# Quarters of turned operands change places in one round of transfers, and the first two groups are loaded once

## The chip, the core and the metric

The kernel runs on one core of a Trainium2 chip. Time is device time of one execution, in microseconds (us), lower is better. Five engines run their own instruction streams in order: TensorE (PE, matmuls), VectorE (DVE), ScalarE (ACT), GpSimd (POOL) and SyncE (SP, which here only issues transfers). Sixteen DMA engines carry the transfers of all queues.

## The reference

Sigmoid attention and two gated MLPs, in float32 (some weights come as float64):

```
scores = q @ k.T / sqrt(64) - log(448)          # q, k, v: 4 batches, 12 heads, 448 x 64
x  = sigmoid(scores) @ v                        # heads side by side: 4 x 448 x 768
h  = relu(x @ w_in);  u, v = halves of h        # 768 -> 2 x 512
x  = (u * (w_spatial @ layernorm(v) + b)) @ w_out
h  = gelu(x @ w_in2); u, v = halves of h
out = x + (u * (w_sg @ (layernorm(v) * g) + b2)) @ w_out2
```

## The kernel before, in words

The work runs in two parts. The first is attention; both MLPs follow, and their matmuls leave PE no gap. The change touches attention alone (the function `attention`).

Attention takes the 48 heads in 12 groups of four. A group has 7 units, one for each 64 keys, so there are 84 units. `scores(n, c)` issues four matmuls for unit c of group n, one for each head, each on a quarter of PE's array (64 rows by 64 columns), and then the sigmoid on ACT. `values(n, c)` issues four more, which add the unit's part to the group's output. In the loop, step s issues the scores of unit s and the values of unit s - LAG, with LAG = 4. In the trace each matmul has two records, so one such set of four is eight records. I call it a **set**. ACT (`gather`) copies a finished group out.

The operands of `scores` need the 64 elements of a head's rows on 64 partitions. `load(n)` brings q and k of a group as 128 rows (4 heads x 32), and `transpose` turns 32x32 blocks on DVE, which puts only 32 elements of each head on 32 partitions of a tile. So `turn(n)` makes two tiles, `even` (elements 0 to 31) and `odd` (32 to 63), and then exchanges quarters: `even[32:64]` (head 1) and `odd[0:32]` (head 0) change places, and so do the quarters 64 partitions on. It copies `even` into a spare tile (L415), sends two transfers from `odd` to `even` (L417), and, because the second pair overwrites what the first reads, sends two more from the spare to `odd` once the first have landed (L419). POOL issues these four transfers. There is one buffer for the spare (`bufs=1`), so the copy of the next group waits until the last pair has landed. There are three buffers for each operand tile and four for what is loaded.

The first two groups go another way: `load_twice` loads each head's rows twice, the second time shifted by 32 elements, so that the transposes (`turn_twice`) put both halves where they belong and nothing is exchanged. SP and ACT issue these loads.

The order of the work is written out: `turn(n + 2)` stands at unit 5 of group n, `load(n + 3)` at unit 3, and `load_v(n + 1)` at unit 0. SP issues q, k and v and the weights of the first MLP in that order, each behind the buffer it fills. On DVE the same program order mixes `turn` with the belt (`convert_early`, L168 to L199): jobs that load a piece of float64 weights and convert it with five to seven DVE instructions; `rate` says when a job starts.

Of the kernel before, what the change touches and what calls it, by code (L numbers as in the profile page):

```python
# [9 lines left out]
F32 = mybir.dt.float32  # L10
# [16 lines left out]
def tile_sigmoid_attention_two_gated_mlps(  # L27
# [32 lines left out]
    nc = tc.nc  # L60
    B, H, S, D = q.shape
    DM = out.shape[2]
    FF = g_ln2.shape[0]
    P = 128
# [3 lines left out]
    TC = S // 32  # L68
# [19 lines left out]
    def chunk_of(b, c):  # L88
        t, c = (xs, c) if c < KF else (xe, c - KF)
        return t[b // 2][:, c * ROW:(c + 1) * ROW + PAD]  # L90
# [253 lines left out]
    for c in range(soon):  # L344
        rows = slice(c * P, (c + 1) * P)
# [7 lines left out]
    def attention(apool, epool, ps_att, ps_last, done):  # L353
        G = H // 4
        NG = B * G

        def place(n):
            b, i = divmod(n, G)
            return b ^ 1, i

        KC = S // 64
        ring, open_sums = [0, 1, 2, 3], {}

        def banks_of(k, name):
            pool = ps_att if k < 3 else ps_last
            return pool.tile([P, 2, 512], F32, tag=f"s{k}", name=name, bufs=1)
        ins, ops, vs, att = {}, {}, {}, {}

        def heads(t, n):
            b, i = place(n)  # L370
            return t[b, 4 * i:4 * i + 4]

        def load_twice(n):


            for w in range(2):
                ins[n, w] = t = apool.tile([P, 2, TC * D], F32, tag="in", name="in", bufs=4)
                src = heads((q, k)[w], n).rearrange("(o x) (t c) d -> o t x (c d)", o=2, c=TC)
                for j in range(2):
                    for o in range(2):  # L380
                        at = 64 * o + 32 * j
                        (nc.sync, nc.scalar)[o].dma_start(
                            out=t[at:at + 32, :, :TC * D - 32 * j], in_=src[o, :, :, 32 * j:]
                        )

        def load(n):
            ins[n] = apool.tile([P, 2, TC * D], F32, tag="in", name="in", bufs=4)
            for w in range(2):
                src = heads((q, k)[w], n).rearrange("h (t c) d -> (h t) (c d)", c=TC)
                nc.sync.dma_start(out=ins[n][:, w], in_=src)  # L390

        def operand(n, x):
            if (n, x) not in ops:
                ops[n, x] = apool.tile([P, 2, S], F32, tag=f"op{x}", name=f"op{x}", bufs=3)
            return ops[n, x]

        def transpose(t, w, src, j=0, chunks=slice(0, None)):
            src = src.rearrange("p (c j d) -> p j c d", c=TC, j=2)[:, j]
            dst = t[:, w]
            if w:  # L400
                src = src.rearrange("p (e c) d -> p c e d", c=KC)[:, chunks]
                dst = dst.rearrange("p (c t e) -> p c e t", c=KC, e=2)[:, chunks]
            else:
                dst = dst.rearrange("p (c t) -> p c t", c=TC)
            nc.vector.transpose(out=dst, in_=src)  # L405

        def turn(n):


            even, odd = [operand(n, x) for x in range(2)]  # L410
            for j, t in enumerate((even, odd)):
                for w in range(2):
                    transpose(t, w, ins[n][:, w], j)
            spare = apool.tile([P, 2, S], F32, tag="ops", name="ops", bufs=1)
            nc.vector.tensor_copy(out=spare, in_=even)  # L415
            for at in (0, 64):
                nc.gpsimd.dma_start(out=even[at + 32:at + 64], in_=odd[at:at + 32])  # L417
            for at in (0, 64):
                nc.gpsimd.dma_start(out=odd[at:at + 32], in_=spare[at + 32:at + 64])  # L419

        def load_v(n):
            vs[n] = vt = epool.tile([P, 2, KC * D], F32, tag="v", name="vt", bufs=3)
            src = heads(v, n)
            row, head = KC * D, S * D
            both = bass.AP(src.tensor, src.offset, [[row, P], [2 * head, 2], [1, row]])
            nc.sync.dma_start(out=vt, in_=both)

        def scores(n, c):


            k = ring.pop(0)
            ring.append(k)
            sc = banks_of(k, "sc")
            for x in range(2):
                for o in range(2):
                    ps, op = slice(64 * o, 64 * o + 64), ops[n, x]
                    nc.tensor.matmul(  # L437
                        sc[64 * x:64 * x + 64, o, :S], op[ps, 1, 64 * c:64 * c + 64], op[ps, 0],
                        start=True, stop=True, tile_position=(64 * o, 64 * x),
                    )  # L440
            att[n, c] = a = epool.tile([P, 2, S], F32, tag="a", name="a", bufs=6)
            nc.scalar.activation(a, sc[..., :S], AF.Sigmoid, bias=bias_s, scale=scale)  # L442

        def values(n, c):


            if n not in open_sums:
                k = ring.pop(0)
                open_sums[n] = k, banks_of(k, "av")
            k, av = open_sums[n]  # L450
            for x in range(2):
                for o in range(2):
                    ps = slice(64 * x, 64 * x + 64)
                    nc.tensor.matmul(  # L454
                        av[o * D:(o + 1) * D, x, :S], vs[n][ps, o, D * c:D * (c + 1)],
                        att[n, c][ps, o], start=(c == 0), stop=(c == KC - 1),
                        tile_position=(64 * x, 64 * o),
                    )
            if c == KC - 1:
                for x in range(2):  # L460
                    gather(n, x, av[:, x])
                ring.append(k)

        def gather(n, x, av):

            b, i = place(n)
            y = chunk_of(b, 2 * i + x)
            o = av[:, :S].rearrange("p (c t) -> p t c", c=TC)

            def back(at, t0, t1):  # L470
                dst = y[:, at:at + (t1 - t0) * TC]
                nc.scalar.copy(out=dst.rearrange("p (t c) -> p t c", c=TC), in_=o[:, t0:t1])

            if b % 2 == 0:
                back(0, 0, 32)
            else:
                t = 3 * P // TC
                back(SPAN, 0, t + 1)
                back(S - 3 * P % TC, t, 32)

        belt.waiting = [convert_early(apool, *x) for x in first]

        units = [(n, c) for n in range(NG) for c in range(KC)]
        U, LAG = len(units), 4

        def rate(p, step):
            if p == 0:
                return int(step in (2, 5))
            return int(step in ((0, 2, 5) if p < NG // 2 - 1 else range(4)))

        load_twice(0)
        load_v(0)
        load_twice(1)
        load(2)
        load_v(1)
        warm = banks_of(ring[-1], "av")[:, 0]
        for _ in range(9):
            nc.tensor.matmul(warm[:, :P], ident, ident, start=True, stop=True)

        def turn_twice(n, w, *chunks):  # L500
            for x in range(2):
                transpose(operand(n, x), w, ins[n, w][:, x], 0, *chunks)

        turn_twice(0, 0)
        for chunks in (slice(0, 1), slice(1, None)):
            turn_twice(0, 1, chunks)
        for s in range(U + LAG):
            n, c = divmod(s, KC)
            if s < U:
                scores(n, c)  # L510
            elif s == U:
                done()
            if s >= LAG:
                values(*units[s - LAG])
            if s in (0, 1):
                turn_twice(1, s)
            if c == 5 and n + 2 < NG:
                turn(n + 2)
            if c == 3 and n + 3 < NG:
                load(n + 3)  # L520
            if c == 0 and 0 < n < NG - 1:
                load_v(n + 1)
            if s % 2 == 0:
                belt.tick(rate(s // 14, s % 14 // 2))
            if s == U:
                load_vecs(l1)
            if s >= U and (s - U) % 2 == 0:
                spatial.tick(1)

        assert open_sums[NG - 1][0] == 3  # L530


    class Mlp:
# [175 lines left out]
        ends = slice(0, 512), slice(512, DM)  # L709
# [103 lines left out]
    with tc.manual_schedule():  # L813
# [4 lines left out]
        apool = tc.tile_pool(name="apool", bufs=1)  # L818
# [13 lines left out]
        with tc.tile_pool(name="epool", bufs=1, side="right") as epool:  # L832
            attention(apool.__enter__(), epool, ps_att.__enter__(), ps_last.__enter__(), operands_made)
# [199 lines left out]
```

## Time and profile before

| | |
|---|---|
| time, median of 3 runs | 579.65 us (577.44 to 581.04) |
| the profiled execution | 580.25 us, span 578.5 us |
| PE busy | 555.5 us, 96% of the span |
| DVE, ACT, POOL busy | 333.5, 219.3, 53.0 us |
| DMA | 62.78 MB, 4.59 MB of them on the queue that POOL issues |
| chain of waits | PE 81%, DMA 13%, other issue 3% |

PE is busy nearly all the time, but this share is a mean over two parts. Where PE has gaps, it is in the first 163 us.

### The profile page before, as it was taken

To read this page: it belongs to the slowest core of one execution; us is meant where nothing else is said; L and a number is where in the kernel's file an instruction comes from. 1 tells how busy PE (TensorE), PEld (TensorE's weight loads), DVE (VectorE), ACT (ScalarE), POOL (GpSimd) and SP (SyncE) were. 2 spreads that over 40 slices of the span, in tenths; PEclk is the share of its full clock that TensorE was granted. 3 is DMA by queue.
4 is the path that set the end of the run, shared out by engine and by line. 5 is a ranking of instruction groups with operands and counts; after the bars stand their busy time and mean duration, and the time that the engine had idled before them with its cause. 6 is when DMAs were issued, how large, how long until landed. Compare 5 with 4: busy or idle time off the path is not lost.

```text
span 578.5 us, 8922 instructions
## 1 busy us (share of the span) xinstructions
PE 555.5 (96%) x3382; PEld 435.9 (75%) x3382; DVE 333.5 (58%) x710; ACT 219.3 (38%) x369; POOL 53.0 (9%) x102
## 2 busy tenths in 40 slices
PE   5959899799999999999999999999999999999997
PEld 4525343233468989889898888999899989999886
DVE  1356675667347969999966597781533065314311
ACT  1726577477744325245253225430321042103101
POOL 0011121212002010020100003000200030001000
PEclk9979899899999999999999999999999999999999
DMA  9996759586233216545345543500230024004103
GB/s 232 316 255 180 199 158 234 134 243 170 76 67 90 91 59 167 121 126 150 95 124 148 130 134 90 153 12 2 37 59 0 1 33 64 1 0 66 17 1 109
DMA packets 90106, 62.78 MB, mean 109 GB/s; under 512 B 63952, under 2 KB 77136, under 8 KB 90064
## 3 DMA queue, kind: packets, MB, share of 16 engines
q1 hardware_dynamic: 88000, 55.56, 37.2%
q0 software_dynamic: 1280, 4.59, 3.2%
q10 hardware_dynamic: 784, 2.06, 1.4%
q8 instruction: 26, 0.43, 0.3%
q14 instruction: 16, 0.13, 0.1%
HBM read 46.60 MB, written 11.01 MB: 100 GB/s over the span
## 4 chain that ended last, share of the span: by engine, by line
PE 81%; DMA 13%; issue 3%; DVE 1%; POOL 0%; SPq 0%; DVEq 0%; POOLq 0%
PE t L562 17%; PE t L608 17%; PE sc L694 10%; PE t L628 6%; DMA op<-ops 6%; PE av L454 5%; PE sc L437 5%; PE av L694 5%; DMA op<-op 4%; PE av L628 3%; PE sc L628 3%; PE sc L704 3%; PE t L790 3%; PE av L790 3%; DMA in<-in_q_dram 2%
## 5 line engine op out<-in xcount | busy, mean ns | idle before, releaser
L437 PE MATMUL sc<-op 64*64 64x448 f32 x672 | 130.5, 573 | 18.2 <-DMA op<-ops 12.9
L454 PE MATMUL av<-a,vt 64*64 64x448 f32 x672 | 124.0, 555 | 0.0
L442 ACT ACTIVATE a<-sc,small 128x896 f32<-128x896 f32 x84 | 84.8, 1013 | 64.7 <-PE sc L437 64.3
L437 PEld LDWEIGHTS sc<-op 64*64 64x64 f32 x672 | 48.9, 142 | 60.5 <-issue 42.7
L454 PEld LDWEIGHTS av<-a,vt 64*64 64x64 f32 x672 | 46.8, 138 | 35.2 <-issue 33.3
L571 DVE BATCH_NORM_STATS2 st<-vr 128x6 f32<-128x512 f32 x28 | 19.4, 694 | 66.8 <-ACT vr L568 66.8
L568 ACT ACTIVATE vr<-t 128x512 f32<-128x512 f32 x28 | 16.7, 597 | 93.9 <-PE t L562 93.9
L573 POOL TENSOR_SCALAR st<-st 128x1 f32<-128x1 f32 x28 | 10.8, 385 | 347.5 <-DVE st L572 347.5
L562 PE MATMUL t<-vh,xh 128*128 128x512 f32 x112 | 41.7, 392 | 0.0
L562 PE MATMUL t<-vh,xl 128*128 128x512 f32 x98 | 38.2, 390 | 0.0
L638 DVE SCALAR_TENSOR_TENSOR gt<-t,bb 128x448 f32<-128x448 f32 x16 | 10.9, 682 | 45.5 <-PE t L628 45.5
L646 ACT CAST gh<-u 128x448 fp32r<-128x448 f32 (+1 forms) x16 | 8.6, 540 | 71.5 <-DVE u L642 71.5
L405 DVE STREAM_TRANSPOSE op<-in 128x448 f32<-128x448 f32 (+2 forms) x50 | 27.2, 599 | 14.7 <-DMA in<-in_q_dram 9.8
L608 PE MATMUL t<-xh,uh 128*128 128x448 f32 x96 | 34.9, 364 | 0.0
L608 PE MATMUL t<-xh,ul 128*128 128x448 f32 x96 | 34.8, 363 | 0.0
L608 PE MATMUL t<-xl,uh 128*128 128x448 f32 x96 | 34.6, 361 | 0.0
L628 PE MATMUL t<-sh,v 128*128 128x448 f32 x112 | 32.8, 363 | 0.0
L562 PE MATMUL t<-vl,xh 128*128 128x512 f32 x84 | 32.7, 390 | 0.0
L550 DVE TENSOR_TENSOR xl<-x,xh 128x512 fp32r<-128x512 f32 (+1 forms) x32 | 20.0, 654 | 20.1 <-ACT xh L549 20.1
L608 PE MATMUL t<-xh,vl 128*128 128x448 f32 x96 | 29.6, 363 | 0.0
L613 ACT ACTIVATE u<-t 128x448 f32<-128x448 f32 x32 | 17.4, 543 | 25.1 <-PE t L608 25.0
L590 ACT CAST v<-vr 128x512 fp32r<-128x512 f32 x24 | 14.9, 622 | 30.5 <-DVE vr L582 30.5
(192 smaller groups left out, 1221.9 us busy)
## 6 DMA issues: line engine op xcount, KB each, us to landing
w<-in_moe_w_in_dram SPq DMA_DIRECT2D x24, 256.0 KB, 2.9
vt<-in_v_dram SPq DMA_DIRECT2D x12, 448.0 KB, 4.6
w<-in_moe_w_out_dram SPq DMA_DIRECT2D x18, 256.0 KB, 3.2
in<-in_q_dram SPq DMA_DIRECT2D x10, 448.0 KB, 6.7
in<-in_k_dram SPq DMA_DIRECT2D x10, 448.0 KB, 8.0
we<-in_moe_w_in_dram SPq DMA_DIRECT2D x12, 256.0 KB, 10.7
we<-in_moe_w_in_dram SPq DMA_DIRECT2D x16, 192.0 KB, 7.3
out_dram<-y SPq DMA_DIRECT2D x48, 56.0 KB, 1.9
```

Of the source, the lines that this page charges most:

```text
L405: nc.vector.transpose(out=dst, in_=src)
L437: nc.tensor.matmul(sc[64 * x:64 * x + 64, o, :S], op[ps, 1, 64 * c:64 * c + 64], op[ps, 0], start=True, stop=True, tile_position=(64 * o, ...
L442: nc.scalar.activation(a, sc[..., :S], AF.Sigmoid, bias=bias_s, scale=scale)
L454: nc.tensor.matmul(av[o * D:(o + 1) * D, x, :S], vs[n][ps, o, D * c:D * (c + 1)], att[n, c][ps, o], start=(c == 0), stop=(c == KC - 1), ti ...
L550: nc.vector.tensor_tensor(out=pair[1][:, :n], in0=src, in1=raw(pair[0][:, :n]), op=ALU.subtract)
L562: nc.tensor.matmul(ps[:, :FF], a, w, start=(c == 0 and n == 0), stop=(c == self.kc - 1 and n == 2),)
L571: nc.vector.bn_stats(out=st, in_=vr)
L608: nc.tensor.matmul(ps[:, :S], w, a, start=(c == 0 and n == 0), stop=(c == self.kc - 1 and n == 2),)
L613: nc.scalar.activation(u, ps[:, :S], AF.Relu if L.n == 1 else AF.Gelu_apprx_tanh)
L628: nc.tensor.matmul(ps[:, :S], a, w, start=(n == 0), stop=(n == len(todo) - 1))
L694: nc.tensor.matmul(self.o[m][:, :n_cols], w, a, start=(not second and i == 0 and n == 0), stop=(second and i == KF - 1 and n == 2),)
L790: nc.tensor.matmul(ps[:, :FF], x, w[:, c], start=(c == 0 and n == 0), stop=(c == KD - 1 and n == 2),)
```

## The change

There are three edits. First, `turn` makes two copies, one of each operand tile (`spares`, tags `t0` and `t1`, one buffer each), and sends all four transfers from the copies, so that none waits for another. Second, groups 0 and 1 are loaded once like the others, by SP alone. Group 1 exchanges its quarters by four copies on DVE. Group 0 is turned by `turn_first`: its transposes write the spare tiles; the first two units (`EARLY`) take their operands from there, in parts of 32 rows that are added up, so that each of these units has eight score matmuls instead of four; meanwhile DVE, ACT and POOL put the exchanged operands together for the units after. Third, `turn(n + 2)` moves from unit 5 to unit 2, and LAG becomes 3, with a table (`sums`) for the first steps.

```diff
--- before.py
+++ after.py
@@ -364,35 +364,28 @@
         def banks_of(k, name):
             pool = ps_att if k < 3 else ps_last
             return pool.tile([P, 2, 512], F32, tag=f"s{k}", name=name, bufs=1)
-        ins, ops, vs, att = {}, {}, {}, {}
+        ins, ops, vs, att, early, EARLY = {}, {}, {}, {}, [], 2
 
         def heads(t, n):
             b, i = place(n)
             return t[b, 4 * i:4 * i + 4]
-
-        def load_twice(n):
-
-
-            for w in range(2):
-                ins[n, w] = t = apool.tile([P, 2, TC * D], F32, tag="in", name="in", bufs=4)
-                src = heads((q, k)[w], n).rearrange("(o x) (t c) d -> o t x (c d)", o=2, c=TC)
-                for j in range(2):
-                    for o in range(2):
-                        at = 64 * o + 32 * j
-                        (nc.sync, nc.scalar)[o].dma_start(
-                            out=t[at:at + 32, :, :TC * D - 32 * j], in_=src[o, :, :, 32 * j:]
-                        )
 
         def load(n):
             ins[n] = apool.tile([P, 2, TC * D], F32, tag="in", name="in", bufs=4)
             for w in range(2):
                 src = heads((q, k)[w], n).rearrange("h (t c) d -> (h t) (c d)", c=TC)
-                nc.sync.dma_start(out=ins[n][:, w], in_=src)
-
-        def operand(n, x):
-            if (n, x) not in ops:
-                ops[n, x] = apool.tile([P, 2, S], F32, tag=f"op{x}", name=f"op{x}", bufs=3)
-            return ops[n, x]
+                ends = (0, 9 * D, TC * D) if (n, w) == (0, 1) else (0, TC * D)
+                for cols in map(slice, ends, ends[1:]):
+                    nc.sync.dma_start(out=ins[n][:, w, cols], in_=src[:, cols])
+
+        def operands(n):
+            ops[n] = [
+                apool.tile([P, 2, S], F32, tag=f"op{x}", name=f"op{x}", bufs=3) for x in range(2)
+            ]
+            return ops[n]
+
+        def spares():
+            return [apool.tile([P, 2, S], F32, tag=f"t{x}", name=f"t{x}", bufs=1) for x in range(2)]
 
         def transpose(t, w, src, j=0, chunks=slice(0, None)):
             src = src.rearrange("p (c j d) -> p j c d", c=TC, j=2)[:, j]
@@ -404,19 +397,48 @@
                 dst = dst.rearrange("p (c t) -> p c t", c=TC)
             nc.vector.transpose(out=dst, in_=src)
 
+        def swaps(ts, us):
+
+
+            for at in (0, 64):
+                yield ts[0][at + 32:at + 64], us[1][at:at + 32]
+                yield ts[1][at:at + 32], us[0][at + 32:at + 64]
+
         def turn(n):
 
 
-            even, odd = [operand(n, x) for x in range(2)]
-            for j, t in enumerate((even, odd)):
+            ts = operands(n)
+            for j, t in enumerate(ts):
                 for w in range(2):
                     transpose(t, w, ins[n][:, w], j)
-            spare = apool.tile([P, 2, S], F32, tag="ops", name="ops", bufs=1)
-            nc.vector.tensor_copy(out=spare, in_=even)
-            for at in (0, 64):
-                nc.gpsimd.dma_start(out=even[at + 32:at + 64], in_=odd[at:at + 32])
-            for at in (0, 64):
-                nc.gpsimd.dma_start(out=odd[at:at + 32], in_=spare[at + 32:at + 64])
+            us = spares()
+            for t, u in zip(ts, us):
+                nc.vector.tensor_copy(out=u, in_=t)
+            for dst, src in swaps(ts, us):
+                if n == 1:
+                    nc.vector.tensor_copy(out=dst, in_=src)
+                else:
+                    nc.gpsimd.dma_start(out=dst, in_=src)
+
+        def turn_first():
+
+
+            ts, us = operands(0), spares()
+            early[:] = us
+            at = ins[0]
+            for j in range(2):
+                transpose(us[j], 0, at[:, 0], j)
+            for j in range(2):
+                transpose(us[j], 1, at[:, 1], j, slice(0, EARLY))
+            for t, u in zip(ts, us):
+                nc.vector.tensor_copy(out=t[:, 0], in_=u[:, 0])
+            for j in range(2):
+                transpose(us[j], 1, at[:, 1], j, slice(EARLY, None))
+            for t, u in zip(ts, us):
+                nc.vector.tensor_copy(out=t[:, 1, 64 * EARLY:], in_=u[:, 1, 64 * EARLY:])
+            for i, (dst, src) in enumerate(swaps(ts, us)):
+                nc.vector.tensor_copy(out=dst[:, 1, 64 * EARLY:], in_=src[:, 1, 64 * EARLY:])
+                (nc.scalar.copy, nc.gpsimd.tensor_copy)[i % 2](out=dst[:, 0], in_=src[:, 0])
 
         def load_v(n):
             vs[n] = vt = epool.tile([P, 2, KC * D], F32, tag="v", name="vt", bufs=3)
@@ -431,13 +453,19 @@
             k = ring.pop(0)
             ring.append(k)
             sc = banks_of(k, "sc")
-            for x in range(2):
-                for o in range(2):
-                    ps, op = slice(64 * o, 64 * o + 64), ops[n, x]
-                    nc.tensor.matmul(
-                        sc[64 * x:64 * x + 64, o, :S], op[ps, 1, 64 * c:64 * c + 64], op[ps, 0],
-                        start=True, stop=True, tile_position=(64 * o, 64 * x),
-                    )
+            parts = [(64, ops[n], 0, 1)]
+            if n == 0 and c < EARLY:
+                parts = [(32, early[j:j + 1] * 2, j, 2) for j in range(2)]
+            for rows, op, j, js in parts:
+                for x in range(2):
+                    for o in range(2):
+                        at = 64 * o if rows == 64 else 64 * o + 32 * x
+                        ps = slice(at, at + rows)
+                        nc.tensor.matmul(
+                            sc[64 * x:64 * x + 64, o, :S], op[x][ps, 1, 64 * c:64 * c + 64],
+                            op[x][ps, 0], start=(j == 0), stop=(j == js - 1),
+                            tile_position=(at, 64 * x),
+                        )
             att[n, c] = a = epool.tile([P, 2, S], F32, tag="a", name="a", bufs=6)
             nc.scalar.activation(a, sc[..., :S], AF.Sigmoid, bias=bias_s, scale=scale)
 
@@ -481,40 +509,35 @@
         belt.waiting = [convert_early(apool, *x) for x in first]
 
         units = [(n, c) for n in range(NG) for c in range(KC)]
-        U, LAG = len(units), 4
+        U, LAG = len(units), 3
+        sums = dict(zip((1, 3, 4), units))
+        sums.update(zip(range(6, U + LAG), units[3:]))
 
         def rate(p, step):
             if p == 0:
                 return int(step in (2, 5))
             return int(step in ((0, 2, 5) if p < NG // 2 - 1 else range(4)))
 
-        load_twice(0)
+        load(0)
         load_v(0)
-        load_twice(1)
+        load(1)
         load(2)
         load_v(1)
         warm = banks_of(ring[-1], "av")[:, 0]
         for _ in range(9):
             nc.tensor.matmul(warm[:, :P], ident, ident, start=True, stop=True)
-
-        def turn_twice(n, w, *chunks):
-            for x in range(2):
-                transpose(operand(n, x), w, ins[n, w][:, x], 0, *chunks)
-
-        turn_twice(0, 0)
-        for chunks in (slice(0, 1), slice(1, None)):
-            turn_twice(0, 1, chunks)
+        turn_first()
         for s in range(U + LAG):
             n, c = divmod(s, KC)
             if s < U:
                 scores(n, c)
             elif s == U:
                 done()
-            if s >= LAG:
-                values(*units[s - LAG])
-            if s in (0, 1):
-                turn_twice(1, s)
-            if c == 5 and n + 2 < NG:
+            if s in sums:
+                values(*sums[s])
+            if s == 0:
+                turn(1)
+            if c == 2 and n + 2 < NG:
                 turn(n + 2)
             if c == 3 and n + 3 < NG:
                 load(n + 3)
```

How the instructions now stand, at three places. Names with a number are buffers: `op0_192` and `op1_193` are the two operand tiles of group 2, `t0_198` and `t1_199` its copies.

POOL, the exchanges of groups 2 and 3 and the first half of the next, before:

```order
L417 DMA op0_206<-op1_207 32x896 x2
L419 DMA op1_207<-ops_212 32x896 x2
L417 DMA op0_316<-op1_317 32x896 x2
L419 DMA op1_317<-ops_322 32x896 x2
L417 DMA op0_434<-op1_435 32x896 x2
```

and now, behind the two copies of group 0:

```order
L441 COPY op1_123<-t0_124 32x448 x2
L421 DMA op0_192<-t1_199 32x896
L421 DMA op1_193<-t0_198 32x896
L421 DMA op0_192<-t1_199 32x896
L421 DMA op1_193<-t0_198 32x896
```

All four read copies, so the third no longer reads or writes what the first two do.

DVE around the exchange of groups 2 and 3, before:

```order
L405 STREAM_TRANSPOSE op1_207<-in_120 128x7x2x32
L415 COPY ops_212<-op0_206 128x896
L175 TENSOR_SCALAR fe_253<-we_192 128x512
L178 TENSOR_SCALAR fe_253<-fe_253 128x512
L181 TENSOR_SCALAR fe_253<-fe_253 128x512
L185 SCALAR_TENSOR_TENSOR fe_253<-we_192,fe_253 128x512
L190 SCALAR_TENSOR_TENSOR fe_253<-we_192,fe_253 128x512
L198 CAST vh1_73<-fe_253 128x512
L199 TENSOR_TENSOR vl1_74<-fe_253,vh1_73 128x512
L405 STREAM_TRANSPOSE op0_316<-in_177 128x448
```

and now (`in_217` is the load of group 3, `we_231` the first piece of weights):

```order
L398 STREAM_TRANSPOSE op1_193<-in_107 128x7x2x32
L416 COPY t0_198<-op0_192 128x896
L416 COPY t1_199<-op1_193 128x896
L175 TENSOR_SCALAR fe_276<-we_231 128x512
L178 TENSOR_SCALAR fe_276<-fe_276 128x512
L181 TENSOR_SCALAR fe_276<-fe_276 128x512
L185 SCALAR_TENSOR_TENSOR fe_276<-we_231,fe_276 128x512
L398 STREAM_TRANSPOSE op0_296<-in_217 128x448
L398 STREAM_TRANSPOSE op0_296<-in_217 128x7x2x32
L398 STREAM_TRANSPOSE op1_297<-in_217 128x448
L398 STREAM_TRANSPOSE op1_297<-in_217 128x7x2x32
L416 COPY t0_302<-op0_296 128x896
```

Two copies stand where one was, and the turn of group 3 comes in the middle of the first weight job instead of behind it.

PE at the start, before:

```order
L498 MATMUL av_125<-ident_63 128x128 x9
L437 MATMUL sc_143<-op0_135 64x448 x2
L437 MATMUL sc_143<-op1_137 64x448 x2
L437 MATMUL sc_154<-op0_135 64x448 x2
L437 MATMUL sc_154<-op1_137 64x448 x2
```

and now:

```order
L528 MATMUL av_112<-ident_63 128x128 x9
L464 MATMUL sc_144<-t0_124 64x448 x4
L464 MATMUL sc_144<-t1_125 64x448 x4
L464 MATMUL sc_169<-t0_124 64x448 x4
L464 MATMUL sc_169<-t1_125 64x448 x4
L482 MATMUL av_180<-a_153,vt_102 64x448 x4
L464 MATMUL sc_185<-op0_122 64x448 x2
```

Units 0 and 1 read the spare tiles with eight matmuls each; the exchanged operands (`op0_122`) are first read by unit 2, behind the values of unit 0.

## Rows read from the trace of the kernel before

**Rows 1.** Busy time by stretches: start:end, length, engines, granted clock, DMA share, GB/s.

```profile
10.79:39.06 28.27, 21.91 (x196) 11.09 (x197) 12.03 (x23) 14.89 (x18) 2.23 (x4) 0.97 1.04 284
39.06:163.23 124.17, 117.61 (x1149) 50.47 (x1149) 75.95 (x156) 81.37 (x106) 18.24 (x36) 0.95 0.65 174
163.23:578.50 415.27, 411.74 (x2021) 370.40 (x2020) 243.93 (x527) 121.56 (x244) 31.80 (x56) 1.00 0.30 74
```

**Rows 2.** Chain of waits, 23 to 54 us: start, length, what.

```profile
23.47 7.07 DMA op<-op
...
31.40 8.60 DMA op<-ops
...
41.32 6.17 DMA op<-op
...
48.55 5.23 DMA op<-ops
```

**Rows 3.** Timeline of PE, where it waited: start, length, instruction, [idle before, releaser].

```profile
39.06 1.99 PE L437 MATMUL sc<-op 64*64 64x448 f32 x3 [6.36 <-DMA op<-ops]
53.82 0.59 PE L437 MATMUL sc<-op 64*64 64x448 f32 x1 [0.86 <-DMA op<-ops]
...
67.33 0.59 PE L437 MATMUL sc<-op 64*64 64x448 f32 x1 [0.99 <-DMA op<-ops]
...
106.02 1.00 PE L437 MATMUL sc<-op 64*64 64x448 f32 x1 [3.13 <-DMA op<-ops]
```

**Rows 4.** Busy time in two stretches of 1 us, columns as in rows 1.

```profile
39.00:40.00 1.00, 0.94 (x2) 0.28 (x2) 0.00 (x0) 0.00 (x0) 0.00 (x0) 0.50 1.03 257
...
107.00:108.00 1.00, 1.00 (x12) 0.32 (x8) 0.93 (x3) 0.13 (x1) 0.70 (x2) 0.50 0.00 0
```

**Rows 5.** Timeline of the start, columns as in rows 3.

```profile
1.35 4.21 PE L498 MATMUL av<-ident 128*128 128x128 f32 x18 [1.35 <-POOL ident masks.py:199]
...
7.11 1.17 DVE L405 STREAM_TRANSPOSE op<-in 128x448 f32<-128x448 f32 x2 [6.22 <-DMA in<-in_q_dram]
...
10.79 6.94 PE L437 MATMUL sc<-op 64*64 64x448 f32 x40 [5.24 <-DVE op L405]
...
12.73 1.01 ACT L442 ACTIVATE a<-sc,small 128x896 f32<-128x896 f32 x1 [10.51 <-PE sc L437]
...
14.22 1.01 ACT L442 ACTIVATE a<-sc,small 128x896 f32<-128x896 f32 x1 [0.49 <-PE sc L437]
...
18.26 0.98 PE L437 MATMUL sc<-op 64*64 64x448 f32 x8
...
30.28 0.98 PE L437 MATMUL sc<-op 64*64 64x448 f32 x8
```

**Rows 6.** Busy time in the first 20 us, columns as in rows 1.

```profile
0.00:4.00 4.00, 2.65 (x12) 2.65 (x13) 0.09 (x2) 1.49 (x2) 0.69 (x6) 1.00 0.55 133
4.00:10.00 6.00, 1.56 (x8) 1.26 (x6) 1.17 (x2) 0.00 (x0) 0.00 (x0) 1.00 1.03 253
10.00:20.00 10.00, 9.21 (x68) 4.79 (x72) 3.74 (x9) 5.64 (x6) 0.00 (x0) 1.00 1.04 290
```

**Rows 7.** Instructions by shape, 0 to 165 us: count, busy us, mean ns, idle before.

```profile
L405 DVE STREAM_TRANSPOSE op<-in 128x448 f32<-128x448 f32 x46 | 25.9, 618 | 12.5 <-DMA in<-in_q_dram 9.8 <-DMA in<-in_k_dram 2.7
...
L415 DVE COPY ops<-op 128x896 f32<-128x896 f32 x10 | 6.2, 619 | 31.9 <-DMA op<-ops 31.9
...
L472 ACT COPY x<-av 128x392 f32<-128x392 f32 x8 | 3.9, 493 | 0.0
...
masks.py:199 POOL TENSOR_SCALAR_AFFINE_SELECT ident<-ident 128x128 f32<-128x128 f32 x1 | 0.3, 292 | 0.1
```

**Rows 8.** Timeline of DVE and POOL, 106 to 110 us, columns as in rows 3.

```profile
106.10 0.63 DVE L415 COPY ops<-op 128x896 f32<-128x896 f32 x1 [7.59 <-DMA op<-ops]
...
107.30 0.98 POOL L417 DMA_DIRECT2D op<-op  x2 [7.63 <-DVE fe L190]
109.89 1.05 POOL L419 DMA_DIRECT2D op<-ops  x2 [1.60 <-PE sc L437]
```

## The prediction

> **What bounds the kernel now.** I read the stages first, then the chain of waits, then what PE waited for, then the prices. From 163.23 us on PE is busy 411.74 of 415.27 us [rows 1]: the MLPs are bound by PE, the change leaves them alone, so whatever the end of attention gains or loses moves the end of the run one for one. In attention the reader is to see two things. The first scores start at 10.79 us, after PE sat idle 5.24 us behind the turned k of group 0 [rows 5]. And the waits of PE are released by the exchange: 6.36 us idle before 39.06, which is unit 14, the first of group 2, and shorter ones before units 21, 28 and 49 at 53.82, 67.33 and 106.02 [rows 3]. In the chain of waits each exchange stands as two rounds, one behind the other: 7.07 and 8.60 us for group 2, 6.17 and 5.23 us for group 3 [rows 2]. The copy into the spare, which must wait until the round before has landed, adds up to 31.9 us of idle DVE [rows 7].
>
> At full pace a unit costs 1.5025 us: the sets of scores at 18.26 and 30.28 us are eight units apart [rows 5]. A unit is two sets, so a set is 0.751 us. At 39.06 the scores of units 14 to 83 (70 sets) and the values of units 10 to 83 (74) are left: 144 x 0.751 = 108.2 us. They took 124.17 us [rows 1]. So 16.0 us are lost behind unit 14, in waits and in the clock after them: the granted clock is 0.50 (1.2 GHz) at 39 us, after 6.36 us idle, and 0.50 at 107 us, after 3.13 us idle [rows 3, 4].
>
> **The change, part by part.** The sum stands on two questions: when unit 14 starts now, and whether anything stops PE behind it.
>
> *Start.* A load of q or k is 448 KB, 0.459 MB. The DMA engines moved 133 GB/s up to 4 us, 253 up to 10 us and 290 up to 20 us at a share of 1.03 to 1.04 [rows 6]: they are full, and the bytes set the times. Of group 0, q was moved twice, 0.90 MB. At these rates that is moved at 5.5 us; the transposes started at 7.11 us [rows 5], so 1.6 us lie between moved and usable. Now q is moved by 3.7 us (the early rate is the least known) and usable at 5.3, the first 9/14 of k at 6.5. The four transposes that unit 0 needs cost 2 x 0.59 for q (1.17 for two [rows 5]) and about 2 x 0.26 for 128 columns of k, by the columns from 0.618 for 448 [rows 7]: first scores near 7.1 us, 3.7 earlier than before.
>
> *Unit 7.* Units 0 and 1 have eight score matmuls each, two sets more. At the start the sigmoids of scores alone stand 1.49 us apart [rows 5], so a set took twice 0.751: PE ran at half pace for about 5.7 us. If it does so again, 3.8 sets are done by 12.8 us. Unit 7 needs 9 sets of scores and 4 of values in front of it, so 9.2 more: 19.7 us. Its operands: DVE does the rest of group 0 (two copies of 448 columns, two transposes and two copies of 320, four copies of 320 columns) at 0.619 for 896 columns and 0.618 for a transpose of 448: 0.66 + 0.94 + 0.5 + 1.0, done at 10.2 us. Group 1 has landed when 2.29 MB are moved, 10.8 + 1.6 = 12.4 us; behind it three transposes, two copies and four copies of 896 columns are 1.85 + 1.24 + 2.48 = 5.6 us: 18.0 us, before 19.7. So group 1 costs nothing; the cover is 1.7 us, and gone if PE starts at full pace. The copies for group 0 on ACT (0.49 each, by 392 columns) and on POOL (about 1.0 each, by 0.292 for 128 columns) [rows 7] are done by 9.6 us, and unit 2 starts behind 12.8. SP's queue now holds all early loads; ACT issues none.
>
> *Unit 14.* q and k of group 2 are usable at 15.6 us (3.21 MB), before DVE is free. From 18.0 us: transposes 2.47, copies 1.24, done at 21.7. Before, POOL issued 0.57 us after such a copy had ended (106.73 to 107.30 [rows 8]): first issue at 22.3 us. The trace has no round of four. It is bounded below by one round of two in the same full stretch, 7.07, and above by two of them in a row, 15.7 us [rows 2]. I take 8.5, near the lower end: the round of two, two more issues of 0.49 (0.98 for two [rows 8]) and half a microsecond for the added bytes, since 0.23 MB is 0.8 us at 290 GB/s. So the operands are there at 30.8 us. PE itself comes to unit 14 at 19.7 + 10.5 = 30.2. Unit 14 starts at 30.8 instead of 39.06: **8.3 us gained**.
>
> *Behind unit 14.* With LAG 3, 143 sets are left, 107.4 us. Does the exchange keep up with 10.5 us a group? One turn of its loop is now two copies (1.24), 0.57 and one round. Rounds of two take 5.23 to 8.60 us [rows 2]; with the added second of issues I take 7.5 on average: 9.3 us. So group 3, whose copies wait for 30.8, is there at 41.1 against 41.3 needed, and from there each group gains about a microsecond of cover. DVE: 75.95 us busy in the old stretch [rows 1] and nine copies more are 81.5 of 107.4 us. DMA: a share of 0.65 over 124.17 us [rows 1] is 81 us of work, 75% of the new stretch. Both have room on the mean. The moves of `turn` to unit 2 and of LAG only shift order; the sigmoid is 1.01 us a unit [rows 5], so the values still find it done. I leave 1 us for short waits: attention ends at 30.8 + 107.4 + 1.0 = 139.2 instead of 163.23. **Gain 24.0 us.**
>
> *Sum.* The profiled execution took 580.25 us, 0.6 above the median of the runs shown: 580.25 - 24.0 = 556.2, so **556 us**.
>
> *A rule against it.* At 107.30 two transfers were issued while DVE was 0.93 busy [rows 4], and the next two were issued at 109.89, 2.59 us later, so the first had landed [rows 8]. The Trainium skill (SBUF — State Buffer, section "SBUF: two separate sides") says that GpSimd cannot write the descriptors of its transfers while a float32 copy on VectorE holds the port that they share. By that rule the two copies and the weight job behind them would hold up each round; as each round starts after its copies, this would be about 1.2 us in front of unit 14 (an estimate: two operations like the copy's 0.62), 557.4 us. The trace shows at most the 0.57 us that are counted above.
>
> **The rivals.** *Four in one round take as long as two rounds.* For it: behind a full queue a round takes 7 to 8.6 us although it moves only 0.23 MB, so it waits behind other transfers, and four may drain no faster. Against it: 2.59 us per round when the queue is empty. Then unit 14 starts at 22.3 + 15.7 = 38.0, and groups 3 to 7 come every 1.8 + 11.4 = 13.2 us, as before (39.06 to 106.02 is 13.4): 1 to 2 us gained, 578 us, no change. Chance 9%.
>
> *In between.* DVE runs in order: a weight job whose load is late holds the next turn, and copies that wait for a round hold the weight jobs. With 12 us a group for groups 3 to 7, 1.5 us over PE's pace, and a clock that falls once or twice after a wait, 8 to 10 us of the gain go: 565 us. Chance 13%. For it: rounds of 8.60 us exist; against it: the room above.
>
> *Slower.* The copies now wait for all four transfers of the group before, and two buffers are held instead of one. If the four drain more slowly than the two rounds did, the loop becomes the bound of all nine groups from 3 on. Unit 77 started before at 163.23 less 18 sets, 149.7 us; now it would at 38.0 + 9 L. Equal at L = 12.4, that is at 10.6 us for four transfers in every group. At 12 us it is 9 x 1.4 = 12.6 us slower, 593 us. For it: 8.60 for two; against it: in the later groups the DMA queue is nearly empty when POOL issues (share 0.00 at 107 us [rows 4]). Chance 5%.
>
> *Start alone.* That the 32-row matmuls of units 0 and 1 are slower than thought changes nothing, as unit 14 waits for its exchange anyway: no case of its own.
>
> **The numbers.** Forecast 73%, by itself 551 to 562 us: 551 if the clock is full from the first scores and the round takes 6.5 us, so that unit 14 starts near 28 and nothing stalls behind it; 562 if the round takes 11 and one clock fall follows. In between 13%, no change 9%, slower 5%. The range 551 to 568 takes in the bounds of the round's price and most of the case in between, and leaves out the last two. A measurement of this kernel tells 1%, 5.8 us, from no change. Faster by more: 73 + 13 = 86%; within: 9%; slower by more: 5%.
>
> **What would show it.** In the new profile: first scores near 7 us; unit 14 near 31 us; one round of four per group in the chain, 7 to 9 us, or none; no idle of PE over 1 us between 31 and 139 us; the granted clock at 1.00 in that stretch; the first MLP's matmuls from about 139 us. The forecast falls if DVE's copies still wait for a round while PE waits for the same one, and it is wrong at its root if the MLPs start at 139 us but the run is not shorter by as much.

## The result and the profile after

The changed kernel takes **556.25 us** (median of 4 runs, 553.74 to 558.28) against 580.35 us before: ratio 0.959, 95% interval 0.9535 to 0.9644. 556 us was forecast. The profiled execution took 556.20 us with a span of 554.4 us. DMA moves 61.02 MB instead of 62.78, and PE is busy 99% of the span instead of 96%.

The stages of the changed kernel, columns as in [rows 1]; the last line answers to the last of [rows 1], the first three to [rows 6]:

```profile
0.00:4.00 4.00, 2.65 (x12) 2.65 (x13) 0.09 (x2) 1.49 (x2) 0.69 (x6) 1.00 0.52 175
4.00:10.00 6.00, 6.00 (x52) 2.99 (x54) 5.68 (x15) 3.14 (x4) 1.23 (x2) 1.00 0.99 348
10.00:20.00 10.00, 10.00 (x111) 5.56 (x107) 8.62 (x16) 6.95 (x8) 0.60 (x1) 1.00 1.04 320
...
40.00:140.00 100.00, 100.00 (x1055) 44.05 (x1048) 74.93 (x155) 75.71 (x97) 17.13 (x32) 1.00 0.70 193
139.01:554.40 415.39, 411.73 (x2020) 370.07 (x2020) 244.55 (x528) 122.16 (x246) 31.80 (x56) 1.00 0.29 74
```

From 40 to 140 us PE is busy all of the time at a granted clock of 1.00 (2.4 GHz), and the MLPs, from 139.01 us on, are what they were (PE is busy 411.73 us here, 411.74 before). So the 24 us come out of the first 163 us of [rows 1].

Every idle time of PE from its first scores to the MLPs, from its timeline; this answers to [rows 3]:

```profile
27.23 0.93 PE L464 MATMUL sc<-op 64*64 64x448 f32 x2 [0.67 <-DMA op<-t]
28.69 1.80 PE L464 MATMUL sc<-op 64*64 64x448 f32 x5 [0.52 <-DMA op<-t]
```

Both belong to unit 14, which has four matmuls of two records each: the first found its operands at 27.23 us, the next two at 28.69. The last started at 29.61 with no idle time in front of it, as PE was at work on the two before it. Behind it PE waits for no exchange again. The clock that follows is in these two stretches:

```profile
28.00:30.00 2.00, 1.48 (x9) 0.47 (x12) 0.31 (x1) 0.00 (x0) 0.00 (x0) 0.95 0.99 232
30.00:33.00 3.00, 3.00 (x20) 1.07 (x16) 2.91 (x6) 1.01 (x1) 1.55 (x3) 0.50 1.05 296
```

The chain of waits has one round of transfers where [rows 2] has four pieces, and the first MLP starts at 139.01 instead of 163.23 us:

```profile
20.62 8.02 DMA op<-t
136.00 3.01 PE av L482 x29
139.01 16.54 PE t L585 x72
```

The start and the first two rounds, from the timeline, as in [rows 5] and [rows 8]:

```profile
4.11 1.56 DVE L398 STREAM_TRANSPOSE t<-in 128x448 f32<-128x448 f32 x4 [3.22 <-DMA in<-in_q_dram]
5.53 3.38 PE L464 MATMUL sc<-t 32*64 32x448 f32 x32
13.23 2.55 DVE L419 COPY op<-t 32x896 f32<-32x896 f32 x4
15.66 1.14 PE L464 MATMUL sc<-op 64*64 64x448 f32 x8
17.96 1.13 DVE L416 COPY t<-op 128x896 f32<-128x896 f32 x2
19.40 2.21 POOL L421 DMA_DIRECT2D op<-t  x4 [11.71 <-DVE t L416]
29.69 1.16 DVE L416 COPY t<-op 128x896 f32<-128x896 f32 x2 [5.45 <-DMA op<-t]
31.45 2.11 POOL L421 DMA_DIRECT2D op<-t  x4 [9.84 <-DVE fe L190]
```

The round of group 2 is issued from 19.40 us on. The chain follows its third transfer, which landed at 28.64 us. The fourth, issued at 21.11, took 8.5 us, the longest of the four, and landed at 29.57; the copies of group 3, which wait for all four, start at 29.69. So the round took 10.2 us.

### The profile page after: what moved, and what is told of

The parts are those of the page before. It is cut to its first block, busy times and chain, and to the rows that moved or that the text cites. A ratio compares the mean times of both kernels' runs of the same rounds, so it can differ in the third digit from the quotient of the medians.

```text
span 554.4 us, 8961 instructions
## 1 busy us (share of the span) xinstructions
PE 548.2 (99%) x3398; PEld 433.4 (78%) x3398; DVE 343.9 (62%) x734; ACT 220.4 (40%) x371; POOL 55.2 (10%) x104
## 2 busy tenths in 40 slices
DMA packets 89547, 61.02 MB, mean 110 GB/s; under 512 B 63776, under 2 KB 77088, under 8 KB 89504
## 4 chain that ended last, share of the span: by engine, by line
PE 94%; DMA 3%; DVE 1%; SPq 0%; issue 0%; POOL 0%
PE t L585 17%; PE t L631 17%; PE av L482 10%; PE sc L717 10%; PE sc L464 10%; PE t L651 6%; PE av L717 5%; PE av L651 3%; PE sc L651 3%; PE sc L727 3%; PE t L813 3%; PE av L813 3%; PE av L727 2%; PE t L727 2%; DMA op<-t 1%; DMA in<-in_k_dram 1%
## 5 line engine op out<-in xcount | busy, mean ns | idle before, releaser
L464 PE MATMUL sc<-op 64*64 64x448 f32 x656 | 120.5, 542 | 1.2 <-DMA op<-t 1.2
L482 PE MATMUL av<-a,vt 64*64 64x448 f32 x672 | 121.1, 542 | 0.0
L464 PEld LDWEIGHTS sc<-op 64*64 64x64 f32 x656 | 44.9, 134 | 38.1 <-issue 31.9
L661 DVE SCALAR_TENSOR_TENSOR gt<-t,bb 128x448 f32<-128x448 f32 x16 | 10.9, 682 | 45.9 <-PE t L651 45.9
L421 POOL DMA_DIRECT2D op<-t x40 | 21.5, 542 | 87.9 <-PE sc L464 58.4
```

Source lines behind the costliest of these rows:

```text
L421: nc.gpsimd.dma_start(out=dst, in_=src)
L464: nc.tensor.matmul(sc[64 * x:64 * x + 64, o, :S], op[x][ps, 1, 64 * c:64 * c + 64], op[x][ps, 0], start=(j == 0), stop=(j == js - 1), tile ...
L482: nc.tensor.matmul(av[o * D:(o + 1) * D, x, :S], vs[n][ps, o, D * c:D * (c + 1)], att[n, c][ps, o], start=(c == 0), stop=(c == KC - 1), ti ...
```

## The experiments

**Which part gives what.** The first four runs, on one chip beside the kernel before (579.38 us median), take the change apart. The theory is the prediction's: an earlier unit 14 through the start, and no waits behind it through the one round. The brackets behind a ratio hold its 95% interval.

*Two rounds in the changed kernel.* In `turn`, for groups 2 to 11:

```diff
-            us = spares()
-            ...  # two copies, four transfers from the copies
+            spare = apool.tile([P, 2, S], F32, tag="t0", name="t0", bufs=1)
+            nc.vector.tensor_copy(out=spare, in_=even)
+            for at in (0, 64):
+                nc.gpsimd.dma_start(out=even[at + 32:at + 64], in_=odd[at:at + 32])
+            for at in (0, 64):
+                nc.gpsimd.dma_start(out=odd[at:at + 32], in_=spare[at + 32:at + 64])
```

> The changed kernel, with the exchange of groups 2 to 11 put back to two rounds (copy of one tile, two transfers, then two more). Theory: the one round is what keeps the groups behind unit 14 from waiting. Then unit 14 starts near 36 us (19.4 + 0.5 + 7 + 9) and groups 3 to 7 come every 12 to 13 us: 566 to 573 us. Rival: the single loads of groups 0 and 1 and the earlier place of the turn do it all, and rounds hide behind the cover of 12 units: 556 to 559 us.

567.04 us, ratio 0.9771 (0.97 to 0.9842). Nearly half of the gain is lost. The two longest waits of PE, from its timeline:

```profile
34.34 1.29 PE L470 MATMUL sc<-op 64*64 64x448 f32 x2 [4.23 <-DMA op<-t]
70.62 0.90 PE L470 MATMUL sc<-op 64*64 64x448 f32 x2 [1.59 <-DMA op<-t]
```

Unit 14 waits 4.23 us more for the second round; later only one wait is above 1 us (two more, before 93.87 and 126.40 us, are 0.98 and 0.56), fewer than the theory had.

*The turn back at unit 5.*

```diff
-            if c == 2 and n + 2 < NG:
+            if c == 5 and n + 2 < NG:
```

> The changed kernel, with the turn back at unit 5 of a group instead of unit 2. Theory: the place only orders DVE, the exchange of group 2 still follows that of group 1 at once, and later groups have cover enough: 555 to 559 us. Rival: the three units of lead (4.5 us) are what the later groups live on; without them each of groups 3 to 7 waits 1 to 3 us: 562 to 570 us.

556.52 us, ratio 0.9594 (0.9524 to 0.9665): the same as the whole change. Its profile has one wait of PE after the first 2 us, 0.27 us at unit 21.

*Both: two rounds and the turn at unit 5.* The two edits above together.

> The changed kernel with two rounds and the turn back at unit 5: of the change, only the start (single loads, group 0 and 1 exchanged by engines) and LAG 3 are left. Theory: the start alone brings unit 14 from 39 to about 36 us, later waits stay: 572 to 577 us. Rival: the start is the larger part of the gain (its bytes free the DMA queue): 560 to 566 us.

571.84 us, ratio 0.9858 (0.9798 to 0.9917). This is the start alone (with LAG 3), and the waits are back:

```profile
33.80 2.19 PE L470 MATMUL sc<-op 64*64 64x448 f32 x3 [6.07 <-DMA op<-t]
59.56 0.59 PE L470 MATMUL sc<-op 64*64 64x448 f32 x1 [0.67 <-DMA op<-t]
71.81 0.93 PE L470 MATMUL sc<-op 64*64 64x448 f32 x2 [1.49 <-DMA op<-t]
73.54 0.68 PE L470 MATMUL sc<-op 64*64 64x448 f32 x1 [0.80 <-DMA op<-t]
99.64 0.59 PE L470 MATMUL sc<-op 64*64 64x448 f32 x1 [2.09 <-DMA op<-t]
```

Against the version with two rounds at unit 2, the place is worth 4.8 us by the medians, and the runs of the two do not overlap (564.66 to 567.95 us, and 569.63 to 572.61). With one round it is worth nothing. So the single round makes the earlier place needless, but not the other way round: the place without the single round still loses 10.5 us (567.04 against 556.52).

*The one round alone, in the kernel before.*

```diff
+            us = [... two tiles t0, t1, one buffer each ...]
+            for t, u in zip((even, odd), us):
+                nc.vector.tensor_copy(out=u, in_=t)
             for at in (0, 64):
-                nc.gpsimd.dma_start(out=even[at + 32:at + 64], in_=odd[at:at + 32])
-            for at in (0, 64):
-                nc.gpsimd.dma_start(out=odd[at:at + 32], in_=spare[at + 32:at + 64])
+                nc.gpsimd.dma_start(out=even[at + 32:at + 64], in_=us[1][at:at + 32])
+                nc.gpsimd.dma_start(out=odd[at:at + 32], in_=us[0][at + 32:at + 64])
```

> The kernel before, with one thing of the change: two copies and all four transfers in one round. Theory: unit 14 starts near 33.5 us (24.2 + 9.2) instead of 39, and the waits behind it go for the most part: 560 to 566 us. Rival: the round is paid in queueing, four together take as long as two rounds behind the doubled loads: 574 to 580 us.

564.77 us, ratio 0.9743 (0.9685 to 0.9802). PE at units 14 and 21, and POOL, from the timeline:

```profile
33.19 1.04 PE L437 MATMUL sc<-op 64*64 64x448 f32 x4 [0.62 <-DMA op<-t]
34.43 0.59 PE L437 MATMUL sc<-op 64*64 64x448 f32 x1 [0.20 <-DMA op<-t]
46.43 0.94 PE L437 MATMUL sc<-op 64*64 64x448 f32 x2 [1.27 <-DMA op<-t]
48.22 1.63 PE L437 MATMUL sc<-op 64*64 64x448 f32 x5 [0.85 <-DMA op<-t]
...
23.52 0.72 POOL L418 DMA_DIRECT2D op<-t  x1 [22.22 <-DVE t L416]
```

Four transfers issued from 23.52 us on let PE go at 34.43: 10.9 us, where the two rounds before took from 23.47 to 40.00 [rows 2]. Put together: the start alone, with LAG 3, gives 579.38 - 571.84 = 7.5 us, the round alone 14.6, both 22.9 (the version with the turn at unit 5). They add up. What of the start's part belongs to the single loads, to the units of eight matmuls or to LAG was not taken apart.

**What is left at unit 14.** The next four ran on one chip beside the kernel before (581.45 us median).

*One warm-up matmul instead of nine.*

```diff
-        for _ in range(9):
+        for _ in range(1):
```

> The changed kernel with one warm-up matmul instead of nine, so that PE is idle from about 2 us to the first scores at 5.5 us. Theory: the first sets then run at half pace, as in the kernel before, and PE comes to unit 14 about 2.5 us later, at 29 instead of 26.5 us; but its operands come at 28.7 us anyway, and there is less idle for the clock to fall after: 555 to 557.5 us. Rival: PE's pace in the first units counts in full: 558 to 560 us.

555.40 us, ratio 0.9557 (0.9524 to 0.9591). The first scores in its timeline:

```profile
5.53 5.40 PE L464 MATMUL sc<-t 32*64 32x448 f32 x32 [3.38 <-DVE t L398]
```

The 32 records of units 0 and 1 took 5.40 us after 3.38 us of idle, and 3.38 us in the changed kernel, where the warm-up runs on until they start. Yet nothing is lost: the MLPs start at 137.61 us. PE comes to unit 14 at 28.20 us and finds its operands there, and the granted clock stays at 1.00. So what the slow start costs here, the changed kernel lost to the wait before unit 14 and the slow clock behind it.

*Group 2 exchanged by copies on DVE.*

```diff
-                if n == 1:
+                if n in (1, 2):
```

> The changed kernel, with group 2 exchanged by four copies on DVE like group 1, so that no transfer stands in front of unit 14. Theory: the last wait in attention is the round of group 2 behind a full DMA queue; without it unit 14 starts at 26.2 us instead of 28.7 and the clock stays at 1.00: 551.5 to 554 us. Rival: the four copies (2.5 us) push the turn of group 3 back on DVE and the wait moves to unit 21: 555 to 558 us.

554.64 us, ratio 0.955 (0.9511 to 0.959). Unit 14 no longer waits and the clock stays at 1.00, but a part of the wait moves to unit 21, whose round is now the first behind the full queue:

```profile
38.84 1.67 PE L464 MATMUL sc<-op 64*64 64x448 f32 x5 [0.47 <-DMA op<-t]
```

The MLPs start at 137.10 us. Theory and rival both had a share, and the median lies between their ranges.

*Groups 2 and 3.* `if n in (1, 2, 3):`

> The same for groups 2 and 3. Theory: no wait before unit 14 nor before unit 21, MLPs from 26.2 + 107.4 = 133.6 to 135 us: 551 to 553 us. Rival: DVE, 5 us fuller, becomes late with the turns of groups 4 and 5 or with the weights: 554 to 558 us.

552.73 us, ratio 0.9499 (0.9469 to 0.9529). No wait of PE for an exchange is left, and the MLPs start at 134.88 us:

```profile
134.88 16.57 PE t L585 x72
```

*Two buffers for each copy.* In `spares`, `bufs=1` becomes `bufs=2`.

> The changed kernel with two buffers for each copy, so that the copies of a group need not wait until the round before has landed (21.3 us of idle DVE in all). Theory: this wait is covered for every group but group 2, whose copies wait for nothing; no change: 555 to 558 us. Rival: the loop of copies and rounds is the bound, or an earlier round of group 3 helps: 550 to 553 us.

554.36 us, ratio 0.9523 (0.9489 to 0.9556). Its profile has no fewer waits: PE is idle three times around unit 14, 0.59, 0.74 and 0.70 us, with the rounds of groups 2 and 3 in the queue together (issued from 19.43 and 27.03 us on). But the profile is of the slowest of six runs (557.29 us); the others took 552.82 to 555.47. The median is a little under what was expected of "no change", and the changed kernel itself did not run beside it. Whether the buffer helps by a microsecond or two stays open.

**Copies in place of transfers.** The last three ran on one chip (before: 580.67 us median), with the changed kernel among them.

*All groups by copies on DVE, no transfer.* `if n >= 1:`

> The changed kernel with every group exchanged by four copies on DVE, and no transfer at all. Theory: the changed kernel's DVE is about 75% busy between 40 and 140 us; eight more groups of 2.5 us make some 96%, so DVE, in order behind late loads, becomes the bound of attention: 556 to 566 us. Rival: DVE still has room, and without 4.6 MB on the DMA queue nothing waits: 550 to 553 us.

*The changed kernel again.*

> The changed kernel as it is, beside the next one on the same chip: 555 to 557 us, with a wait before unit 14 in the profile.

*Groups 2 and 3 again.*

> The changed kernel with groups 2 and 3 exchanged by copies on DVE, once more. Theory: 2.5 to 4 us less than the changed kernel in the same call. Rival: what it seemed to gain was the other chip's: less than 1 us apart.

553.13 us (ratio 0.952, 0.9491 to 0.9549) without any transfer, 558.85 (0.9607, 0.9571 to 0.9644) for the changed kernel, and 554.42 (0.9548, 0.9514 to 0.9582) with groups 2 and 3 on DVE. The theory on the first was wrong. Busy times from 40 to 137 us, in the version without transfers and in the first profile of the changed kernel, and where the former's MLPs start:

```profile
40.00:137.00 97.00, 96.30 (x1012) 61.25 (x1005) 90.46 (x181) 71.79 (x92) 0.00 (x0) 1.00 0.49 151
```

```profile
40.00:137.00 97.00, 97.00 (x1037) 42.37 (x1033) 72.57 (x151) 72.71 (x91) 17.13 (x32) 1.00 0.72 196
```

```profile
135.74 16.88 PE t L585 x72
```

DVE (the third busy time) is 90.46 of 97 us busy, 93% where some 96% were reckoned, and it still came in time: the MLPs start at 135.74 us, and PE waits for no exchange. The version without transfers is clear of the changed kernel, 5.7 us by the medians, and the intervals do not meet; between it and the version with groups 2 and 3 on DVE nothing is decided. The interval of the latter touches the changed kernel's, so its 4.4 us are likely, not certain. That is a little more than the 2.5 to 4 us expected, and the expectation for the changed kernel was 2 us low: its profile here has more idle time at unit 14 than the first time.

```profile
28.92 0.93 PE L464 MATMUL sc<-op 64*64 64x448 f32 x2 [1.39 <-DMA op<-t]
30.61 1.75 PE L464 MATMUL sc<-op 64*64 64x448 f32 x5 [0.76 <-DMA op<-t]
```

## Why the prediction was right, step by step

**What bounds the kernel**: right. The exchange released PE's waits, and the time of the MLPs did not move.

**Start**: mis-sized by 1.6 us. First scores at 5.53 us instead of 7.1. The bytes were reckoned at the rates of [rows 6], 133 and 253 GB/s; the single loads were moved at 175 and 348 at about the same shares. So the first transposes could start at 4.11 instead of 5.3 us. (By its own rate q is moved by 3.45 us and not 3.7; k came later in the sum, so the forecast does not hang on it.)

**Unit 7**: the step that failed was "if it does so again", PE at half pace for 5.7 us. In this profile PE ran at full pace from the first scores, right behind the warm-up, and unit 7 started at 15.66 us, not 19.7. The cover that I named as gone in this case was gone: DVE's last copy for group 1 ended at 15.78, 0.1 us behind the start of unit 7, though PE shows no idle time there. The version with one warm-up matmul shows that a slow start costs nothing in the end. (The rest of group 0 on DVE adds up to 2.8 us by the prices named and not to 3.1; it took 3.7, 5.59 to 9.25 us, and still ended before the k of group 1 was there, at 10.45.)

**Unit 14**: 28.69 us instead of 30.8, and 29.61 for its last matmul. The round is issued at 19.40 instead of 22.3, as all before it came earlier. But it takes 10.2 us, so the 8.5 of the sum was 1.7 too small: the price lies nearer the middle of its bounds than the lower end. The issue, 2.9 us early, covered that, which is luck too. The rival that four take as long as two rounds falls with 10.2 and 10.9 against 16.5 us. And PE was at unit 14 earlier than I had it, at about 26.2 us, one set behind 25.43, so most of the unit waits 2.5 us.

**Behind unit 14**: 139.01 - 28.69 = 110.3 us instead of 108.4. There are no waits for an exchange, as forecast, but the last matmul of unit 14 is 0.9 us behind, and the clock is 0.50 for some 3 us after the wait before unit 14. I had forecast a wait there of 0.6 us and no fall of the clock. The 2.1 us that the start came early and the 1.9 us that were lost here cancel: that attention ends at 139.0 and not at 139.2 us is luck in the last two microseconds, not in the rest. The spread between runs fits in part: the run of 553.74 us has a mean clock of 1.000, those of 556.2 and 558.28 us of 0.997 and 0.993; the second time this kernel took 554.21 and 554.92 us at 1.000, and 558.83 to 559.91 at 0.994 to 0.997. But with the turn at unit 5 two runs took 558.47 and 558.80 us at 1.000 and 0.999, so the clock is not all of it. Nor did each such wait bring the clock down: with the round alone PE was idle 1.27 and 0.85 us around 47 us, and the granted clock read 1.00 from 46 to 52 us.

**The exchange's loop**: right, though group 3 is there at 40.1 us by the prediction's own 30.8 + 9.3, and not at 41.1; its round had landed at 39.85. The rounds behind group 2 took 5.8 to 10.5 us, 7.4 on average, against 7.5 reckoned. They go out at 31.45, 41.71, 52.59 and 63.63 us, 10 to 11 us apart, PE's own pace. DVE's copies still wait for rounds (21.3 us in all, 31.9 before [rows 7]), without PE waiting. With one round the place of `turn` cost and gave nothing, which the version with the turn at unit 5 shows; LAG alone was not tried.

**The rule against it.** The first round was issued 0.31 us after its copies had ended (19.09 to 19.40), with DVE idle behind them; the second 0.60 us after (30.85 to 31.45), with DVE at work. The Trainium skill (SBUF — State Buffer, section "SBUF: two separate sides") has GpSimd shut out while a float32 copy on VectorE holds the port. The 0.3 us agree with it in sign, and with nothing like the 1.2 us reckoned by it. Nor do they follow the length of the operation behind the copy: in the kernel before, the issue came 0.57 to 0.59 us after the copy in all nine rounds with DVE at work, behind operations of 0.35 to 0.69 us. What the 0.3 us are stays open; the version without transfers cannot tell them apart from the queue. But at the start, in the turn of group 0, copies of the two engines do get in each other's way:

```profile
6.98 0.28 DVE L438 COPY op<-t 128x320 f32<-128x320 f32 x1
6.99 0.69 POOL L441 COPY op<-t 32x448 f32<-32x448 f32 x1
7.18 0.68 DVE L438 COPY op<-t 128x320 f32<-128x320 f32 x1
```

The second of two like copies on DVE took 0.68 us instead of 0.28 and ended 0.2 us behind POOL's copy, and so it did in all eleven profiles that have these copies. That is 0.4 us once, and DVE's wait for the k of group 1 takes it up.

**The other rivals.** "In between" and "slower" did not come: no wait behind unit 14, and DVE came in time even at 93%.

## What to carry to other kernels

Where two rounds of transfers depend on each other only because the second overwrites what the first reads, a copy of both sides makes them one round, and the price is the copy. Before relying on cover, see what the transfer waits behind: four small transfers took 10.2 us at a DMA share of 1.05, where two sent into the empty queue had landed 2.59 us later [rows 8], and copies on an engine with room did the same work with no queue at all. Parts that follow each other on the way to the same unit add up (the start has the round issued earlier, the single round makes it shorter); a part that only gives cover for a wait (the place) is worth nothing once another has taken the wait away.

## What the runs showed of the hardware

What sets the pace of PE at the start is not settled. The same 32 records of units 0 and 1, right behind the same nine warm-up matmuls, took 3.38 us in the first profile of the changed kernel, 4.09 in the second and 4.16 with the turn at unit 5, though PE had no idle time in front of them; after one warm-up matmul and 3.38 us of idle they took 5.40. The granted clock reads 1.00 in all four stretches. The line of the second profile:

```profile
5.53 4.09 PE L464 MATMUL sc<-t 32*64 32x448 f32 x32
```

But where the start is that of the kernel before (one round alone, 5.21 us of idle), it reads 0.50, the lower of the two levels, for the slow scores:

```profile
10.00:16.00 6.00, 5.22 (x28) 2.64 (x32) 2.34 (x6) 2.32 (x3) 0.00 (x0) 0.50 1.05 298
```

So a 1.00 at the start of a profile does not show full pace; look at how long the matmuls take. And loads of 128 rows from one queue were moved at 348 GB/s at a DMA share of 0.99, where loads of 32 partitions from two queues had 253 at 1.03 [rows 6]; whether the shape or the queues make the difference is not shown.
